# Dealing out a triangular solve over two chunks, with single-operation masks and a range check on one engine

## The chip, the cores and the metric

The kernel runs on one core of one Trainium2 chip. The metric is the device time of one execution in microseconds (us). TensorE (PE, matmuls), VectorE (DVE), ScalarE (ACT), GpSimd (POOL) and the DMA queue of SyncE (SP) each run their own instruction stream in order and wait for each other through semaphores.

## The reference

Three steps follow one another. The first is a recurrence with a state of 40 x 40 for each of 4 x 8 heads over 768 time steps; its output `y` goes through an MLP (320 to 2048 to 320), and that through a mixture of eight experts whose gates come from eight rounds of row and column normalisation.

```python
for t in range(S):                       # S = 768, state: [B=4, H=8, 40, 40]
    y[:, :, t] = einsum('bhd,bhde->bhe', rt, state)
    Sa = einsum('bhde,bhe->bhd', state, at)
    state = state * wt[:, :, None, :] - einsum('bhd,bhe->bhde', Sa, bt) \
            + einsum('bhd,bhe->bhde', vt, kt)
...
h = x @ w_in                             # 3072 x 320 @ 320 x 2048
g = where(h > 0, h, exp(min(h, 0)) - 1)
x = g @ w_out
...
for e in range(8):
    out += P[:, e:e+1] * (maximum(x @ w1[e], 0) @ w2[e])
```

## The kernel before

The 768 steps are cut into 24 chunks of 32. Within a chunk the recurrence becomes matmuls and, for each head, the solution of a 32 x 32 unit triangular system. Its coefficients come from a masked product (E3: matmuls, mask, store to DRAM as `Ad`, and step LT, which loads them as `LT` in the layout of the solve). The solve is `tsolve`: VectorE alternates a multiply (L417, `Tt<-Wk,LT`) and an update of `Wk` (L424) through 31 columns, 62 operations, for two chunks at once, and then SP stores `Wk` to DRAM (`Td`, L430) and loads it back transposed (`TT`, L434), the operand of the matmuls of step H2 (L463).

One turn of the main loop is one chunk c. A string in `PLAN["order"]` sets the order of its steps: prep (VectorE clamps and scans L312 to L322, GpSimd products L324, L333, L334, ScalarE's sum of squares L336 for the range check of w), E1 to E4, H1 to H4, O1 to O3b, `x` and `xl` (transposes of the finished y, `X` L576), and `m`, one unit of the first MLP (matmuls `ph` L588, ScalarE `m` L590 and L591, VectorE `g` L597, ScalarE `gh` L599, GpSimd `gl` L601, matmuls L615 to L619). O2 masks a product into `Gm` (L368), which O3b's matmuls (L545) read; O3a (L534) is between them; then comes VectorE's `xT` (L548). H3 ends with VectorE's `Y` (L494), which H4 (L503) reads.

At an even c, `T` creates the solve for chunks c+2 and c+3 and makes its first step, the start values of `Wk`. `G` allows it to be pumped from there on; every `p` then issues `PLAN["tp"]` operations of it, 3 in an even turn and 4 in an odd one. There are 16 places `p` in a turn. From c=4 on, the order on TensorE, VectorE, ScalarE and GpSimd is pinned as written; what stands on SP's queue, and everything before c=4 (`PLAN["start"]`), is ordered by a scheduler. After the last chunk, stage two runs the eight experts.

Of the kernel before, what the change touches and what calls it, by code (L numbers as in the profile page):

```python
# [98 lines left out]
def build(ctx, tc, r, k, v, w, a, b, w_in, w_out, wg, w1, w2, wa_d, kb_d, re_d, ro_d, vt_d, wp_d, consts, out, C, off):  # L99
# [140 lines left out]
    TTs = [r1.tile([128, H, 64], F32, name=f"TT{i}") for i in range(4)]  # L240
# [16 lines left out]
    def rec_init():  # L257
        for t in (wr, wq, dr, dq):
            V.memset(t, 0.0)
        work[1] = (early(1, "wr", [4 * NG, C + 1]), early(1, "wq", [4 * NG, C]), early(1, "dq", [4 * NG, C]), early(1, "aB", [NG * 2 * 2, 64]).rearrange("p (g u j) t -> p g u j t", u=2, j=2))  # L260
        for t in work[1]:
            G.memset(t, 0.0)
        V.memset(dr[:, :, 0], 1.0)
        for i in (3, 2):
            V.memset(bank[i], 0.0)
        for t in (aB, wmm, rB, *Ams, *TTs, Yw, Gm):
            G.memset(t, 0.0)
        for i in (0, 1):
# [134 lines left out]
    def tsolve(*cs):  # L403
        n = len(cs)
        LT2 = ltp[cs[0]][0]
        x0 = ltp[cs[0]][1]
        Wk = r1.tile([128, 2, CI, C], F32, tag="Wk", name="Wk")
        tmp = r1.tile([128, 2 * CI * (C - 1)], F32, tag="Tt", name="Tt")
        for x in range(n):
            G.tensor_copy(out=Wk[:, x].rearrange("p i t -> p (i t)"), in_=idk)  # L410
# [599 lines left out]
    with ExitStack():  # L1010
# [179 lines left out]
```

## Time and profile before

| | |
|---|---|
| device time, median of 3 runs | 2341.04 us (2337.09 to 2345.46) |
| profiled execution | 2338.0 us, span 2336.2 us |
| mean granted clock of TensorE | 0.976 |
| busy share of the span: PE, DVE, ACT, POOL | 92%, 43%, 31%, 22% |
| chain that ended last | PE 73%, DVE 15%, DMA 4% |

The span runs from the first to the last instruction. A share is a mean over stages: the start (to about 284 us) has the weight conversion and the first chunks, the middle (to about 825 us) the loop described above, and the rest the experts. The chain is followed back from the last instruction, each time to what released it. The granted clock is the share of TensorE's full speed (2.4 GHz) that it was given.

### The profile page before, as it was taken

To read this page: it belongs to the slowest core of one execution; us is meant where nothing else is said; L and a number is where in the kernel's file an instruction comes from. 1 tells how busy PE (TensorE), PEld (TensorE's weight loads), DVE (VectorE), ACT (ScalarE), POOL (GpSimd) and SP (SyncE) were. 2 spreads that over 40 slices of the span, in tenths; PEclk is the share of its full clock that TensorE was granted. 3 is DMA by queue.
4 is the path that set the end of the run, shared out by engine and by line. 5 is a ranking of instruction groups with operands and counts; after the bars stand their busy time and mean duration, and the time that the engine had idled before them with its cause. 6 is when DMAs were issued, how large, how long until landed. Compare 5 with 4: busy or idle time off the path is not lost.

```text
span 2336.2 us, 47201 instructions
## 1 busy us (share of the span) xinstructions
PE 2160.3 (92%) x19908; PEld 1967.2 (84%) x19908; DVE 1005.3 (43%) x2160; ACT 734.9 (31%) x1639; POOL 507.3 (22%) x608
## 2 busy tenths in 40 slices
PE   2376899999999999999999999999999999999998
PEld 2266888888888999899999999999999999999997
DVE  7888766666777522542222222222222222222222
ACT  3243455445455456323212112112112112112111
POOL 6344344434444326001002002002002002001000
PEclk9997899989999999999999999999999999999999
DMA  5353333333333214201001001001001001000000
GB/s 156 94 137 102 93 99 96 94 98 85 91 95 95 66 44 120 60 1 32 19 1 38 13 1 38 13 1 44 7 1 45 6 1 47 4 1 20 23 23 24
DMA packets 168452, 118.60 MB, mean 51 GB/s; under 512 B 102632, under 2 KB 148200, under 8 KB 168232
## 3 DMA queue, kind: packets, MB, share of 16 engines
q1 hardware_dynamic: 168232, 115.50, 18.5%
q8 instruction: 158, 2.59, 0.5%
q14 instruction: 62, 0.51, 0.1%
HBM read 96.97 MB, written 18.48 MB: 49 GB/s over the span
## 4 chain that ended last, share of the span: by engine, by line
PE 73%; DVE 15%; DMA 4%; ACT 3%; issue 2%; POOL 2%; SPq 1%; DVEq 0%; ACTq 0%; POOLq 0%
PE h L773 30%; PE pa L815 9%; PE pa L814 9%; PE pa L813 9%; PE ph L588 5%; DVE Tt L417 4%; DVE Wk L424 4%; PE a L615 1%; DVE g L597 1%; DMA WA<-in_wa 1%; PE a L616 1%; PE a L617 1%; PE P L364 1%; PE P L545 1%; DMA raw<-in_moe_w_out 1%
## 5 line engine op out<-in xcount | busy, mean ns | idle before, releaser
L773 PE MATMUL h<-X,a 128*128 128x512 f32 x3072 | 775.5, 394 | 0.0
L773 PEld LDWEIGHTS h<-X,a 128*128 128x128 f32 x3072 | 564.0, 188 | 102.8
L777 DVE SCALAR_TENSOR_TENSOR hl<-h,hh 128x512 fp32r<-128x512 f32 x384 | 264.8, 690 | 875.9 <-ACT hh L776 875.7
L776 ACT ACTIVATE hh<-h 128x512 fp32r<-128x512 f32 x384 | 230.0, 600 | 1021.2 <-PE h L773 1017.6
L814 PE MATMUL pa<-a,hl 128*128 128x320 f32 x1536 | 474.7, 310 | 0.0
L813 PE MATMUL pa<-a,hh 128*128 128x320 f32 x1536 | 472.1, 308 | 0.7 <-ACT acc L820 0.4
L815 PE MATMUL pa<-a,hh 128*128 128x320 f32 x1536 | 468.4, 309 | 0.0
L814 PEld LDWEIGHTS pa<-a,hl 128*128 128x128 f32 x1536 | 288.7, 188 | 16.0
L813 PEld LDWEIGHTS pa<-a,hh 128*128 128x128 f32 x1536 | 288.8, 188 | 15.6 <-ACT acc L820 0.8
L741 POOL TENSOR_TENSOR a<-rw,a 128x384 fp32r<-128x384 f32 x64 | 65.1, 1018 | 1057.8 <-ACT a L739 1050.5
L815 PEld LDWEIGHTS pa<-a,hh 128*128 128x128 f32 x1536 | 287.3, 188 | 0.0
L588 PE MATMUL ph<-X,Wt 128*128 128x256 f32 x1536 | 233.7, 296 | 16.0 <-DVE g L597 14.9
L601 POOL TENSOR_TENSOR gl<-g,gh 128x256 fp32r<-128x256 f32 x192 | 161.0, 839 | 381.0 <-ACT gh L599 278.5
L588 PEld LDWEIGHTS ph<-X,Wt 128*128 128x128 f32 x1536 | 202.6, 196 | 21.8 <-DVE g L597 17.1
L597 DVE SCALAR_TENSOR_TENSOR g<-m,ph 128x256 f32<-128x256 f32 x192 | 80.0, 416 | 176.8 <-ACT m L591 172.8
L417 DVE TENSOR_TENSOR Tt<-Wk,LT 128x120 f32<-128x120 f32 (+30 forms) x403 | 144.2, 358 | 25.7 <-POOL Wk L410 12.0
L424 DVE TENSOR_TENSOR Wk<-Wk,Tt 128x120 f32<-128x120 f32 (+30 forms) x403 | 145.5, 361 | 11.6
L824 DVE SCALAR_TENSOR_TENSOR acc<-pa,Pg,acc 128x320 f32<-128x320 f32 x168 | 84.3, 544 | 114.8 <-PE pa L815 114.8
L599 ACT ACTIVATE gh<-g 128x256 fp32r<-128x256 f32 x192 | 80.0, 417 | 163.4 <-DVE g L597 161.9
L590 ACT ACTIVATE m<-ph 128x256 f32<-128x256 f32 x192 | 73.2, 381 | 158.7 <-PE ph L588 156.6
L591 ACT ACTIVATE m<-m 128x256 f32<-128x256 f32 x192 | 80.1, 417 | 5.7
L615 PE MATMUL a<-gh,WoB 128*128 128x256 f32 x216 | 69.5, 322 | 1.3 <-ACT gh L599 1.3
(169 smaller groups left out, 2340.8 us busy)
## 6 DMA issues: line engine op xcount, KB each, us to landing
LT<-Ad SPq DMA_DIRECT2D x24, 512.0 KB
rw<-in_moe_w SPq DMA_DIRECT2D x64, 160.0 KB
WA<-in_wa SPq DMA_DIRECT2D x24, 416.0 KB
KE<-in_kb SPq DMA_DIRECT2D x24, 416.0 KB
rw<-in_moe_w SPq DMA_DIRECT2D x64, 128.0 KB
VU<-in_vt SPq DMA_DIRECT2D x24, 320.0 KB
raw<-in_wp SPq DMA_DIRECT2D x16, 384.0 KB
raw<-in_moe_w_out SPq DMA_DIRECT2D x16, 320.0 KB
```

Source lines behind the costliest of these rows:

```text
L417: V.tensor_tensor(out=tv, in0=Wk[:, 0:n, 0:ni, j:j + 1].to_broadcast(sh), in1=LT2[:, x0:x0 + n, j, j + 1:C].unsqueeze(2).to_broadcast(sh), ...
L424: dve["T"] = V.tensor_tensor(out=Wk[:, 0:n, 0:ni, j + 1:C], in0=Wk[:, 0:n, 0:ni, j + 1:C], in1=tv, op=ALU.subtract)
L588: T.matmul(ph, lhsT=Wt[0:kp, wi, 128 * f:128 * f + 128], rhs=X[0:kp, xi, :], start=(i == 0), stop=(i == 7))
L597: V.scalar_tensor_tensor(out=g, in0=m, scalar=-1.0, in1=ph, op0=ALU.add, op1=ALU.max)
L601: G.tensor_tensor(out=gl, in0=g, in1=gh.bitcast(F32), op=ALU.subtract)
L615: T.matmul(o, lhsT=Wo(f)[:, 128 * i:128 * i + 128], rhs=gh, start=(s and i == 0), stop=False, skip_group_check=True)
L773: T.matmul(h, lhsT=a1[:, wi, :], rhs=X[bk][:, xi, :], start=(i == 0), stop=(i == 7))
L776: A.activation(out=hh, in_=h, func=AF.Relu)
L777: V.scalar_tensor_tensor(out=hl, in0=h, scalar=0.0, in1=hh.bitcast(F32), op0=ALU.max, op1=ALU.subtract)
L813: T.matmul(o, lhsT=hh[:, ts_], rhs=a2[:, 0, :], start=(f == 0), stop=False)
L814: T.matmul(o, lhsT=hl[:, ts_], rhs=a2[:, 0, :], start=False, stop=False)
L815: T.matmul(o, lhsT=hh[:, ts_], rhs=a2[:, 1, :], start=False, stop=(f == NF2 - 1))
```

## The change

- The first operations of a solve are dealt earlier: `G` stands between the two halves of H3 in place of behind O2, and `PLAN["tp"]` alternates, 3 and 3 operations in an even turn, 2 and 3 in an odd one.
- The coefficients of three chunks lie in one tile, used in turn (`c % 3`), and LT always stands at its first place in the string. The start values of `Wk` come by a DMA from the constants, not by GpSimd copies; there are two `TT` tiles, not four.
- A mask is one VectorE operation over 128 partitions and 1024 elements that also writes the zeroes; the clearing of the mask tiles at the start is gone.
- The range check: GpSimd's subtraction L334 and ScalarE's Square are replaced by two ScalarE passes, Abs of w less the middle of the range, and Relu of that less half the range, summed.

```diff
-    "order": "lv E4 m prep+3 ldw+4 p E3+3 xl m E3+3 p H1 m p E2+3 LT+3 m p H2 lu+1 m prep+4 p E1+3 ldk+4 m prep+4 p x m T prep+4 p H3 m x H3 p O1 m O1 p H4 m YW+1 prep+4 p O2 x m O2 G p m x p O3a m prep+4 p O3b m O3b p m p m p LT+3 w",
+    "order": "lv E4 m prep+3 ldw+4 p E3+3 xl m E3+3 p H1 m p E2+3 LT+3 m p H2 lu+1 m prep+4 p E1+3 ldk+4 m prep+4 p x m T prep+4 p H3 m G x H3 p O1 m O1 p H4 m YW+1 prep+4 p O2 x m O2 p m x p O3a m prep+4 p O3b m O3b p m p m p w",
-    "tp": (3, 4),
+    "tp": ((3, 3), (2, 3)),
-    TTs = [r1.tile([128, H, 64], F32, name=f"TT{i}") for i in range(4)]
+    TTs = [r1.tile([128, H, 64], F32, name=f"TT{i}") for i in range(2)]
-        for t in (aB, wmm, rB, *Ams, *TTs, Yw, Gm):
+        for t in (aB, wmm, rB, *TTs, Yw):
             G.memset(t, 0.0)
...
-        G.tensor_tensor(out=wv, in0=wv, in1=wr[0:HR, :, 1:C + 1][:, :, ::-1], op=ALU.subtract)
-        yield
-        A.activation(out=wf, in_=wf, func=AF.Square, accum_out=wmm[0:HR, c:c + 1])
+        yield
+        A.activation(out=wf, in_=wf, func=AF.Abs, bias=wmid[0:HR])
+        A.activation(out=wf, in_=wf, func=AF.Relu, bias=whalf[0:HR], accum_out=wmm[0:HR, c:c + 1])
...
-        for bi in range(2):
-            p, q = slice(64 * bi, 64 * bi + 64), slice(C * bi, C * bi + C)
-            V.tensor_tensor(
-                out=dst[p].rearrange("p u h t -> p (u h) t")[:, :, q],
-                in0=PS[p, :].rearrange("p (h t) -> p h t", t=C),
-                in1=cc("mask")[p, q].unsqueeze(1).to_broadcast([64, 2 * H, C]),
-                op=ALU.mult,
-            )
+        V.tensor_tensor(
+            out=dst.rearrange("p u h (b t) -> p (u h) b t", b=2),
+            in0=PS.rearrange("p (h t) -> p h t", t=C).unsqueeze(2).to_broadcast([128, 2 * H, 2, C]),
+            in1=cc("mask").rearrange("p (b t) -> p b t", b=2).unsqueeze(1).to_broadcast([128, 2 * H, 2, C]),
+            op=ALU.mult,
+        )
...
-        LT2 = ltp[c - 1][0] if x else r1.tile([128, 2, C, C], F32, tag="LT", name="LT")
-        ltp[c] = (LT2, x)
-        SY.dma_start(out=LT2[:, x].rearrange("p s t -> p (s t)"), in_=dap(z.Ad, 0, [[C * C, B * H], [0, 4], [1, C * C]]))
+        SY.dma_start(out=LTs[:, c % 3].rearrange("p s t -> p (s t)"), in_=dap(st[c].Ad, 0, [[C * C, B * H], [0, 4], [1, C * C]]))
...
-        for x in range(n):
-            G.tensor_copy(out=Wk[:, x].rearrange("p i t -> p (i t)"), in_=idk)
+        SY.dma_start(out=Wk[:, 0:n].rearrange("p x i t -> p x (i t)"), in_=consts[:, nidk:nidk + CI * C].unsqueeze(1).to_broadcast([128, n, CI * C]))
...
-                        solve(PLAN["tp"][c % 2])
+                        pk += 1
+                        solve(PLAN["tp"][c % 2][pk % 2])
```

The line numbers of the changed kernel are a little lower: L417 becomes L412, L424 L419, L430 L425, L434 L429, L393 L389, L494 L489, L439 L434, L597 L592, L548 L543 on VectorE and L553 L548 on SP; the new Wk load is L405. The order of the matmuls in the loop stays as it was.

Place 1 is VectorE's stream in an even turn, from Y on: where a solve begins. Before:

```order
L494 TENSOR_TENSOR Y<-P_99,Yw 104x8x40
L494 TENSOR_TENSOR Y<-P_100,Yw 104x8x40
L597 SCALAR_TENSOR_TENSOR g<-m,ph 128x256
L439 COPY uE<-P_102 80x512
L597 SCALAR_TENSOR_TENSOR g<-m,ph 128x256
L368 TENSOR_TENSOR Gm<-P_101,cst 64x16x32 x2
L417 TENSOR_TENSOR Tt<-Wk,LT 128x62
L424 TENSOR_TENSOR Wk<-Wk,Tt 128x2x31
L417 TENSOR_TENSOR Tt<-Wk,LT 128x60
L576 TENSOR_TENSOR X<-P_102,X 128x3x128
```

The same stretch in the changed kernel, from the second Y on:

```order
L489 TENSOR_TENSOR Y<-P_100,Yw 104x8x40
L412 TENSOR_TENSOR Tt<-Wk,LT 128x62
L419 TENSOR_TENSOR Wk<-Wk,Tt 128x2x31
L412 TENSOR_TENSOR Tt<-Wk,LT 128x60
L592 SCALAR_TENSOR_TENSOR g<-m,ph 128x256
L434 COPY uE<-P_102 80x512
L419 TENSOR_TENSOR Wk<-Wk,Tt 128x2x30
L412 TENSOR_TENSOR Tt<-Wk,LT 128x58
L419 TENSOR_TENSOR Wk<-Wk,Tt 128x2x29
L412 TENSOR_TENSOR Tt<-Wk,LT 128x56
L419 TENSOR_TENSOR Wk<-Wk,Tt 128x2x28
L412 TENSOR_TENSOR Tt<-Wk,LT 128x108
```

Right behind these come g and the mask Gm, three further operations of the solve, and X: nine operations of the solve have moved ahead of Gm, from the odd turn.

Place 2 is VectorE's stream near the end of the odd turn, where a solve ends. Before:

```order
L597 SCALAR_TENSOR_TENSOR g<-m,ph 128x256
L368 TENSOR_TENSOR Gm<-P_101,cst 64x16x32 x2
L417 TENSOR_TENSOR Tt<-Wk,LT 128x32
L424 TENSOR_TENSOR Wk<-Wk,Tt 128x16x2
L417 TENSOR_TENSOR Tt<-Wk,LT 128x16
L424 TENSOR_TENSOR Wk<-Wk,Tt 128x16
L597 SCALAR_TENSOR_TENSOR g<-m,ph 128x256
L548 TENSOR_TENSOR xT<-P_101,xT 128x160
L548 TENSOR_TENSOR xT<-P_102,xT 128x160
```

And in the changed kernel:

```order
L592 SCALAR_TENSOR_TENSOR g<-m,ph 128x256
L368 TENSOR_TENSOR Gm<-P_101,cst 128x1024
L412 TENSOR_TENSOR Tt<-Wk,LT 128x70
L419 TENSOR_TENSOR Wk<-Wk,Tt 128x2x7x5
L412 TENSOR_TENSOR Tt<-Wk,LT 128x56
L419 TENSOR_TENSOR Wk<-Wk,Tt 128x2x7x4
L412 TENSOR_TENSOR Tt<-Wk,LT 128x48
L592 SCALAR_TENSOR_TENSOR g<-m,ph 128x256
L419 TENSOR_TENSOR Wk<-Wk,Tt 128x16x3
L412 TENSOR_TENSOR Tt<-Wk,LT 128x32
L543 TENSOR_TENSOR xT<-P_101,xT 128x160
L543 TENSOR_TENSOR xT<-P_102,xT 128x160
```

Ten operations of the solve stand behind Gm now, in place of four, and the last three come behind xT.

Place 3 is SP's queue from the end of one solve to the load of the coefficients for the next. Before:

```order
L430 DMA Td<-Wk 256x1x32 x6
L434 DMA TT_109<-Td 32x8x32 x4
L430 DMA Td<-Wk 256x1x32 x2
L553 DMA yd<-xT 128x384
L304 DMA rO<-in_ro 104x512
L434 DMA TT_110<-Td 32x8x32 x4
L287 DMA WA<-in_wa 104x1024
L565 DMA yt<-yd 128x384
L383 DMA Ad<-Am_118 32x8x32 x4
L393 DMA LT<-Ad 128x1x1024
L292 DMA KE<-in_kb 104x1024
```

In the changed kernel:

```order
L425 DMA Td<-Wk 256x1x32 x2
L548 DMA yd<-xT 128x384
L425 DMA Td<-Wk 256x1x32 x4
L429 DMA TT_109<-Td 32x8x32 x4
L425 DMA Td<-Wk 256x1x32 x2
L289 DMA WA<-in_wa 104x1024
L560 DMA yt<-yd 128x384
L429 DMA TT_110<-Td 32x8x32 x4
L383 DMA Ad<-Am_117 32x8x32 x4
L405 DMA Wk<-in_consts 128x2x256
L294 DMA KE<-in_kb 104x1024
L389 DMA LT<-Ad 128x1x1024
```

The store of y (yd) now stands among the stores of the solve, and the Wk load and the load of KE stand ahead of LT.

## Rows read from the trace of the kernel before

**Rows 1.** Busy time by window: us, then busy us (instructions) by engine, clock, DMA share, GB/s

```profile
core 0: us, PE busy (x) PEld busy (x) DVE busy (x) ACT busy (x) POOL busy (x), PEclk, DMA share, GB/s
284.00:825.00 541.00, 498.83 (x8533) 467.15 (x8533) 373.87 (x898) 272.57 (x703) 224.29 (x266) 0.96 0.35 90
825.00:2336.00 1511.00, 1496.44 (x8993) 1356.55 (x8991) 406.19 (x723) 361.58 (x696) 154.15 (x175) 1.00 0.08 24
```

**Rows 2.** Waits of TensorE from 284 to 825 us

```profile
engine line waited for: us in total, times, longest us
PE P L534 <- ACT m L591: 18.7, 9, 2.2
PE P L503 <- DVE Y L494: 9.3, 7, 1.3
PE ph L588 <- DVE g L597: 7.2, 8, 1.6
```

**Rows 3.** Timeline of TensorE, its waits in one pair of turns

```profile
start us, us, engine line op out<-in xcount [idle before <-releaser]
660.42 0.49 PE L534 MATMUL P<-Ss,rO 40*32 40x40 f32 x32 [0.64 <-DVE X L576]
...
682.34 1.22 PE L588 MATMUL ph<-X,Wt 128*128 128x256 f32 x8 [0.79 <-DVE g L597]
...
686.72 0.98 PE L503 MATMUL P<-cst,Yw 104*128 104x104 f32 x8 [1.33 <-DVE Y L494]
...
694.09 1.06 PE L534 MATMUL P<-Ss,rO 40*32 40x40 f32 x64 [2.20 <-ACT m L591]
```

**Rows 4.** Busy time by window around the odd turn of that pair

```profile
663.00:695.00 32.00, 27.68 (x485) 25.93 (x480) 30.14 (x75) 16.22 (x43) 13.30 (x15) 0.99 0.26 71
...
690.00:695.00 5.00, 2.80 (x80) 2.61 (x79) 4.65 (x14) 2.50 (x6) 1.74 (x2) 0.94 0.16 36
695.00:700.00 5.00, 5.00 (x62) 4.65 (x54) 0.97 (x3) 0.70 (x2) 4.16 (x5) 0.72 0.54 140
```

**Rows 5.** Timeline of VectorE, odd turn

```profile
662.70 0.79 DVE L548 TENSOR_TENSOR xT<-P,xT 128x160 f32<-128x160 f32 x2 [0.68 <-PE P L545]
...
665.13 1.14 DVE L424 TENSOR_TENSOR Wk<-Wk,Tt 128x104 f32<-128x104 f32 x1
...
666.52 0.25 DVE L417 TENSOR_TENSOR Tt<-Wk,LT 128x100 f32<-128x100 f32 x1
...
692.60 1.39 DVE L368 TENSOR_TENSOR Gm<-P,cst 64x512 f32<-64x512 f32 x2
```

**Rows 6.** Timeline of VectorE, even turn

```profile
652.42 0.88 DVE L494 TENSOR_TENSOR Y<-P,Yw 104x320 f32<-104x320 f32 x2
...
656.87 0.42 DVE L597 SCALAR_TENSOR_TENSOR g<-m,ph 128x256 f32<-128x256 f32 x1 [2.50 <-ACT m L591]
...
659.81 0.56 DVE L576 TENSOR_TENSOR X<-P,X 128x384 fp32r<-128x384 f32 x1
```

**Rows 7.** Timeline of GpSimd

```profile
655.19 1.25 POOL L456 TENSOR_TENSOR Yw<-Y,Wf 104x640 f32<-104x640 f32 x1
...
664.93 1.22 POOL L334 TENSOR_TENSOR WA<-WA,wr 104x512 f32<-104x512 f32 x1
```

**Rows 8.** The load of the coefficients: its issue on SP, and one on the chain

```profile
648.97 0.56 SPq L393 DMA_DIRECT2D LT<-Ad  x1
...
45.01 3.48 DMA LT<-Ad
```

**Rows 9.** Timelines and chain between the last step of a solve and H2

```profile
245.03 0.18 DVE L424 TENSOR_TENSOR Wk<-Wk,Tt 128x16 f32<-128x16 f32 x1
...
253.27 1.22 PE P L463 x30
...
632.23 1.45 PE L545 MATMUL P<-KB,Gm 128*64 128x40 f32 x32
...
644.30 0.90 PE L463 MATMUL P<-RH,TT 64*64 64x40 f32 x24
```

**Rows 10.** Timeline of ScalarE behind its pass L336 of the even turn

```profile
641.21 0.38 ACT L590 ACTIVATE m<-ph 128x256 f32<-128x256 f32 x1 [2.01 <-PE ph L588]
```

**Rows 11.** Start: timelines of GpSimd and of VectorE

```profile
12.37 3.52 POOL L334 TENSOR_TENSOR WA<-WA,wr 104x512 f32<-104x512 f32 x2
...
221.12 0.22 DVE L417 TENSOR_TENSOR Tt<-Wk,LT 128x62 f32<-128x62 f32 x1 [4.85 <-POOL Wk L410]
```

More of the change, by code (lines that the diff above doesn't have):

```diff
@@ L250, in build @@
     rB = r1.tile([128, NG, 2, 2, 64], F32, name="rB")
-    wmm = per.tile([128, NCH], F32, name="wmm")
+    wmm = per.tile([128, NCH + 2], F32, name="wmm")
+    wmid, whalf = wmm[:, NCH:NCH + 1], wmm[:, NCH + 1:NCH + 2]
     CI = C // 4
-    idk = r1.tile([128, CI * C], F32, name="idk")
     work = {None: (wr, wq, dq, aB)}
@@ L265, in rec_init @@
             V.memset(bank[i], 0.0)
-        for t in (aB, wmm, rB, *Ams, *TTs, Yw, Gm):
+        for t in (aB, wmm, rB, *TTs, Yw):
             G.memset(t, 0.0)
+        G.memset(wmid, -(WLO + WHI) / 2)
+        G.memset(whalf, 1e-5 - (WHI - WLO) / 2)
         for i in (0, 1):
@@ L384, in E3 @@
         z.Ad = Ad
-    ltp = {}
+    LTs = r1.tile([128, 3, C, C], F32, name="LT")
     def LT(c):
-        z = st[c]
-        x = c % 2
-        LT2 = ltp[c - 1][0] if x else r1.tile([128, 2, C, C], F32, tag="LT", name="LT")
-        ltp[c] = (LT2, x)
-        SY.dma_start(out=LT2[:, x].rearrange("p s t -> p (s t)"), in_=dap(z.Ad, 0, [[C * C, B * H], [0, 4], [1, C * C]]))
+        SY.dma_start(out=LTs[:, c % 3].rearrange("p s t -> p (s t)"), in_=dap(st[c].Ad, 0, [[C * C, B * H], [0, 4], [1, C * C]]))
     def E4(c):
@@ L404, in tsolve @@
         n = len(cs)
-        LT2 = ltp[cs[0]][0]
-        x0 = ltp[cs[0]][1]
+        x0 = cs[0] % 3
+        LT2 = LTs[:, x0:x0 + n] if x0 + n <= 3 else LTs[:, ::-2]
         Wk = r1.tile([128, 2, CI, C], F32, tag="Wk", name="Wk")
         tmp = r1.tile([128, 2 * CI * (C - 1)], F32, tag="Tt", name="Tt")
-        for x in range(n):
-            G.tensor_copy(out=Wk[:, x].rearrange("p i t -> p (i t)"), in_=idk)
+        SY.dma_start(out=Wk[:, 0:n].rearrange("p x i t -> p x (i t)"), in_=consts[:, nidk:nidk + CI * C].unsqueeze(1).to_broadcast([128, n, CI * C]))
         yield
@@ L419, in tsolve @@
                 in0=Wk[:, 0:n, 0:ni, j:j + 1].to_broadcast(sh),
-                in1=LT2[:, x0:x0 + n, j, j + 1:C].unsqueeze(2).to_broadcast(sh),
+                in1=LT2[:, :, j, j + 1:C].unsqueeze(2).to_broadcast(sh),
                 op=ALU.mult,
@@ L430, in tsolve @@
                 SY.dma_start(out=Td.rearrange("x (i q) t -> q x i t", q=4)[q], in_=Wk[q::4, x])
-            z.TT = TTs[c % 4]
+            z.TT = TTs[c % 2]
             for bb in range(B):
@@ L704, in check_w @@
         mm = c1.tile([128, 1], F32, name="mmw")
-        V.tensor_reduce(out=mm, in_=wmm, axis=AX.X, op=ALU.add)
+        V.tensor_reduce(out=mm, in_=wmm[:, 0:NCH], axis=AX.X, op=ALU.add)
         V.tensor_scalar(out=mm, in0=mm, scalar1=0.0, scalar2=None, op0=ALU.is_le)
@@ L1013, in build @@
         SY.dma_start(out=cst, in_=consts[:, 0:ncst])
-        SY.dma_start(out=idk, in_=consts[:, nidk:nidk + CI * C])
         SY.dma_start(out=wgs[:, 0:2, :], in_=wg[0:256, :].rearrange("(k p) e -> p k e", p=128))
@@ L1117, in build @@
                     step("T" if n == "t" else n, cs[0])
-        acc = 0
+        acc = pk = 0
         for c in range(2, NCH + 1):
@@ L1136, in build @@
                     try_xprep(n == "xl")
-                elif n == "LT":
-                    if not pump:
-                        advance(n, c + o)
                 elif n == "T":
```

2 rows, old and new, of the table PLAN are left out of this document.

## The prediction

> **What bounds the kernel now.** I read the busy times by stage first, then TensorE's waits in the stage with the gaps, then the timeline around one of each wait, and only then the other engines there. The last stage, after 825 us, is 1496 of 1511 us TensorE at full clock [rows 1]; the change doesn't touch it. The middle stage, 284 to 825 us, has 499 of 541 us of TensorE at a mean granted clock of 0.96 [rows 1]: here the recurrence runs two chunks per turn, woven with the first MLP. TensorE's waits there come in a few kinds only [rows 2]: 18.7 us at L534 in 9 waits, 9.3 at L503 and 7.2 at L588 behind g, 35.2 us together.
>
> One turn shows where they sit. In the odd chunk TensorE stops 0.79 us for g, 1.33 for Y and 2.20 before L534 [rows 3]. The last is put down to ACT's m, but L534 starts at 694.09, just when VectorE's second Gm mask ends (692.60 plus 1.39, [rows 5]); L545 reads Gm right behind, in the same step of the order, so I take the mask as the releaser. VectorE is busy 30.1 of 32 us in this odd chunk [rows 4], with solve steps between everything else: it is the bound of this stretch, and only of it. In the even chunk it has 2.50 us idle before one g [rows 6].
>
> Behind the 2.20 us wait the granted clock falls: 0.94 in the five us with the wait, 0.72 in the next five [rows 4], so toward the lower level (1.2 of 2.4 GHz). That costs 5 x (0.06 + 0.28) = 1.7 us per turn. Nine waits make 15 us; the stage's mean says 541 x 0.04 = 22, rounded. I use 19. The waits of 0.64 in the even chunk, and of 0.79 and 1.33 in the odd one [rows 3], come before the fall, with 0.99 as mean of the 32 us around them [rows 4].
>
> **Part by part.** *Solve steps dealt anew.* 62 steps per pair: 18 in the even and 44 in the odd chunk before, 27 and 35 after. Between the even chunk's xT and the odd chunk's Gm stand 15 fewer steps: 9 at the front, and 6 at the end, now behind Gm (order, places 1 and 2). An undisturbed step there takes 0.25 us and the next begins at about 0.29 [rows 5]; 9 x 0.3 + 6 x 0.25 = 4.2 us.
>
> *Range check off GpSimd.* L334 took 1.22 us on GpSimd from 664.93, and the step that began at 665.13 took 1.14 in place of 0.25 [rows 5, 7]. Without L334 that is 0.9 us back, or nothing if the multiply before it merely moves there. ScalarE gets one more pass per chunk over the same tile, bounded by GpSimd's 1.22 us for it; right after its old pass it waits 2.01 us for TensorE [rows 10], which covers that. Without the cover m and then g would be up to 1.2 us later.
>
> *One mask operation.* Two of 512 elements end in 1.39 us; two xT additions of 160 took 0.79 [rows 5]: 0.85 ns per element by that slope, so one of 1024 is 1.13, against no saving at all as the other bound. I take 1.2, a gain of 0.2.
>
> Together 4.2 + 0.9 + 0.2 = 5.3 us; Gm would begin at 687.3. With no waits TensorE would come to that L534 at 694.09 - 2.20 - 1.33 - 0.79 = 689.77, and bring Gm's input 2.1 us earlier than before, which then sets Gm to about 687.7 and its end to 688.9: 0.9 us to spare. If L334's 0.9 stays, the spare is near nothing, but no wait of note comes. So the odd waits go: **-35 us**, and with the 2.20 wait the fall of the clock: **-19 us**.
>
> *What the even chunk pays.* Nine more steps are 2.3 us, into an idle time of 2.50 [rows 6]. But the first step needs the coefficient load LT. It was issued at 648.97 before [rows 8]; in the new order the Wk load and the solve's end stand ahead of it on the queue of SP (order, place 3), which I put at three issues of LT's own 0.56 us, 1.7 in all; with 3.5 us for the load (an early one, [rows 8]) it lands near 654.2, while VectorE comes to the step when Y is done, at 653.3 [rows 6]. Behind that step in VectorE's order are g, uE, the other steps, Gm, and then, after three further ones, X, for which L534 already waits 0.64 us [rows 3]. X begins at 659.81 now [rows 6], also behind three steps; 0.9 of waiting and 2.3 of steps, less 2.5 of idle and 0.2 of the mask, gives +0.5 for X. Two of the moved steps also meet GpSimd's Yw (1.25 us at 655.19, [rows 7]); if it holds them as L334 held its step, X is 0.9 later still. The bounds for this wait are no growth and +1.4 per turn; I take 0.8, eight times: **+6 us**.
>
> Row 665.13 shows a two-input VectorE operation lasting exactly as long as the GpSimd operation beside it runs on [rows 5, 7]. The Trainium skill ("SBUF — State Buffer", section "SBUF: two separate sides") says that the port pair shared by VectorE and GpSimd is locked for a whole instruction, for VectorE operations with two SBUF inputs against a GpSimd operation that reads SBUF. That speaks against moving steps into GpSimd's Yw; by the rule alone the even term would be the 1.4 bound, 11 us in place of 6.
>
> *Coefficients to H2.* The last step now stands behind xT in the odd chunk. The path from last step to H2 took 253.27 - 245.21 = 8.1 us early in the run [rows 9]. L545 ends at 633.68 and H2 begins at 644.30 [rows 9]: 10.6 us. Less xT 0.8, three steps 0.6, the yd store issued between the Td stores 0.5 leaves 8.7 against 8.1, and part of the 10.6 was slow clock that goes. So it is thin: between 0 and 0.8 us of wait, **+3 us** for eight turns.
>
> *Wk by a load, two TT tiles, ring of three.* The load replaces a copy on GpSimd; its time lies under LT's, counted above. Only the first step of a solve waits for either. A TT tile is read by H2 before the next solve of the same parity ends. Nothing.
>
> *The first pair and a remainder:* c=4 isn't yet in step; one wait with its fall of the clock may stay: **+2 us** (one of 2.2 plus 1.7, half likely). *Start, before 284 us:* two L334 (3.52 us, [rows 11]) and some memsets are gone ahead of the first keys, worth 0 to 3.5 us; the solve that begins at 221.12 after 4.85 us idle [rows 11] waits for a load (3.5 us as a bound by LT, [rows 8]) in place of a copy, and its order is moved past a mask: 0 to 3.5 lost. I take **-1**.
>
> Sum: -35 - 19 + 6 + 3 + 2 - 1 = -44. The profiled execution took 2338.0 us (span 2336.2), 3.0 below the median of the three runs: 2338 - 44 = **2294**.
>
> **Rivals.** *The waits move to the even chunk.* LT lands late and Yw holds steps: X is 1.4 later, L534 waits 2.0 us, and the clock falls there in place of the odd chunk. 8 x (0.6 + 1.7) = 18 more: 2312. For it: the idle time is nearly used up. Against: 0.5 follows from undisturbed rows.
>
> *The clock keeps falling though the waits are short.* Several small waits per turn stay by the terms above. Against it speak those of 0.64, 0.79 and 1.33 that left it high [rows 3, 4]. If not: 8 x 1.7 = 14, 2308. The Trainium skill ("TensorE: Matmul & The Clock Gate", section "A second HAM failure mode: psum-queue depth-cycling") has frequent micro-idles between groups of matmuls as enough to make the clock go up and down.
>
> *Slower: the coefficients come late for H2.* Td, TT and yd share SP's queue with the loads, in order. From the forecast, 44 / 8 = 5.5 us per turn, with a fall of the clock 3.8 of wait, are needed to lose everything. If yd's wait for xT holds the four Td stores and TT behind them, H2 comes 6 us late: 8 x (6 + 1.7) = 62, 2356. Against: the spare of about 0.6 would have to be wrong by 4.
>
> *No change.* Gm isn't the releaser of L534, and the steps only change place: the odd waits stay, 2338.
>
> *Better.* X not later, the start's gain whole: 2338 - 35 - 22 - 3 = 2278.
>
> **How the numbers follow.** Forecast (2283 to 2303) 0.52; waits in the even chunk 0.24; clock 0.07; better 0.05; slower 0.07; no change 0.05. The range, 2278 to 2320, holds the first four: about 0.85. About 0.3% (7 us) is what a measurement here tells from no change: faster 0.88, same 0.05, slower 0.07.
>
> **What would show it.** In 284 to 825: the waits at L534's, L503's and L588's counterparts in the odd chunk under 0.4 us, mean clock 0.99 or more, the stage about 43 us shorter. Masks of 1.2 us in one row. The first step of a solve waiting about 1 us for LT or Wk, and X's wait near 1.2 in the even chunk. Wrong would be: a wait of 2 us at any place in each turn, H2 waiting for TT, or an odd L534 that still starts when Gm ends.

## The result and the profile after

The changed kernel took 2352.81 us against 2336.99 us (medians of 14 runs each): 1.006 times as long, 95% interval 1.0049 to 1.0071. The forecast was 2294. The profiled execution has a span of 2350.8 us, 14.6 more than before. The first matmul of the expert stage stands at 894.44 us before and at 903.01 after, so 8.6 us are lost ahead of that stage and 6.0 within it, though the diff changes no matmul of it.

The 8.6 us don't lie in the eight pairs of turns from chunk 4 to chunk 19. Counted from the first matmul of H2 (L463 before, L458 after), these take 523.2 us before and 522.9 after: the odd turns are 46.5 us shorter in all (288.8 to 242.3), the even ones 46.1 longer (234.5 to 280.6). Lost are 4.5 us ahead of chunk 4's H2 (252.3 and 256.8) and 4.4 between chunk 20's H2 and the expert stage, where the last solve begins in the same late way (turn 20 takes 27.7 us before and 33.1 after).

The same two views as in [rows 1] and [rows 2], busy time by window and TensorE's waits from 284 to 825 us:

```profile
core 0: us, PE busy (x) PEld busy (x) DVE busy (x) ACT busy (x) POOL busy (x), PEclk, DMA share, GB/s
0.00:284.00 284.00, 158.05 (x2188) 136.17 (x2188) 212.53 (x514) 101.60 (x230) 112.20 (x143) 0.66 0.44 118
284.00:825.00 541.00, 501.22 (x8580) 469.08 (x8578) 373.26 (x861) 289.11 (x731) 208.03 (x235) 0.97 0.37 95
```

```profile
engine line waited for: us in total, times, longest us
PE P L366 <- DVE uE L434: 16.6, 7, 3.0
PE P L529 <- ACT m L585: 5.6, 7, 0.8
PE P L529 <- DVE X L571: 4.5, 7, 0.7
PE P L529 <- ACT m L586: 3.5, 3, 1.3
PE P L458 <- DMA TT<-Td: 3.4, 7, 0.8
```

The start's clock, 0.66 here and 0.89 in the trace before, belongs to the execution and not to the kernel: in the sixteen traces of this document it is 0.66 to 0.69 in six and 0.86 to 0.89 in ten, and chunk 4's H2 starts at 251.5 to 262.7 us in the six and at 250.4 to 257.3 in the ten.

The waits of the odd turn are gone or short, as forecast: nothing for Y or g, and 0.8 us left ahead of O3a (L529, before L534). In their place TensorE waits up to 3.0 us for uE, in the even turn. The next three views follow one pair of turns: TensorE's rows, a window of five us, and VectorE in the even turn.

```profile
649.40 0.28 PE L458 MATMUL P<-RH,TT 64*64 64x40 f32 x2 [0.65 <-ACT m L585]
649.84 1.09 PE L458 MATMUL P<-RH,TT 64*64 64x40 f32 x30 [0.16 <-DMA TT<-Td]
...
664.16 0.69 PE L366 MATMUL P<-rB,uE 80*64 80x64 f32 x16 [2.16 <-DVE uE L434]
...
683.08 1.13 PE L458 MATMUL P<-RH,TT 64*64 64x40 f32 x32
...
699.56 0.78 PE L529 MATMUL P<-Ss,rO 40*32 40x40 f32 x64 [0.81 <-ACT m L585]
...
713.81 1.50 PE L458 MATMUL P<-RH,TT 64*64 64x40 f32 x32 [0.57 <-DMA TT<-Td]
```

```profile
664.00:669.00 5.00, 4.84 (x67) 4.64 (x67) 4.76 (x12) 3.55 (x9) 2.73 (x3) 0.66 0.16 36
```

```profile
657.78 0.88 DVE L489 TENSOR_TENSOR Y<-P,Yw 104x320 f32<-104x320 f32 x2
662.44 0.22 DVE L412 TENSOR_TENSOR Tt<-Wk,LT 128x62 f32<-128x62 f32 x1 [3.78 <-DMA LT<-Ad]
...
663.43 0.68 DVE L434 COPY uE<-P 80x512 f32<-80x512 f32 x1
...
664.94 1.18 DVE L419 TENSOR_TENSOR Wk<-Wk,Tt 128x58 f32<-128x58 f32 x1
...
667.18 1.22 DVE L368 TENSOR_TENSOR Gm<-P,cst 128x1024 f32<-128x1024 f32 x1
```

The first step of the solve waits 3.78 us for LT, with g, uE and Gm behind it on VectorE; TensorE waits 2.16 us for uE, and the granted clock falls to 0.66 in the five us behind that. From one H2 (L458) to the next, the even turn shown takes 33.7 us and the odd one 30.7. Before, the matmuls of L463 began at 644.30 [rows 9] and at these times, so the turns took 29.4 and 35.4:

```profile
673.73 1.13 PE L463 MATMUL P<-RH,TT 64*64 64x40 f32 x32
...
709.15 1.13 PE L463 MATMUL P<-RH,TT 64*64 64x40 f32 x32
```

The pair is about as long as it was: the loss has changed turns.

Why LT is late, from SP's queue:

```profile
650.15 1.79 SPq L429 DMA_DIRECT2D TT<-Td  x4
651.99 2.19 SPq L383 DMA_DIRECT2D Ad<-Am  x4
654.25 0.43 SPq L405 DMA_DIRECT2D Wk<-in_consts  x1
654.77 0.38 SPq L294 DMA_DIRECT2D KE<-in_kb  x1
655.62 0.56 SPq L389 DMA_DIRECT2D LT<-Ad  x1
```

LT is issued at 655.62 and the step starts at 662.44, 6.8 us later; the prediction had taken 3.5 for the load. Its 512 KB stand behind 256 KB of start values and 416 KB of KE. Means of the eight even turns, counted from H2's start, give the whole of it: LT is issued at 7.9 us (5.0 before), the step starts at 13.8, and it waits 3.7 us. The issue is late because of the Ad store ahead of it, which LT reads back: the mask that makes its data ends at least 3.0 us ahead of H2, but the store is issued behind the solve's last TT load, here 2.6 us behind H2's start (before: 0.1 us ahead of it).

The expert stage shows its loss in the distance of its units (8 matmuls of L768, L773 before, and 12 more). Block 0 of the tokens, then block 1, in the changed kernel; then block 1 before:

```profile
1468.61 2.00 PE L768 MATMUL h<-X,a 128*128 128x512 f32 x8
1472.20 1.09 PE L768 MATMUL h<-X,a 128*128 128x512 f32 x4
...
1497.34 2.04 PE L768 MATMUL h<-X,a 128*128 128x512 f32 x8
1500.98 2.04 PE L768 MATMUL h<-X,a 128*128 128x512 f32 x8
```

```profile
1487.08 2.02 PE L773 MATMUL h<-X,a 128*128 128x512 f32 x8
1490.70 2.02 PE L773 MATMUL h<-X,a 128*128 128x512 f32 x8
```

A unit of block 0 takes 3.59 us in both kernels (before: 1458.35 to 1461.94), one of block 1 takes 3.61 to 3.62 before and 3.64 after, at full clock and with TensorE never idle. Blocks 2 to 5 do as block 1. The change also adds two columns to the tile `wmm`, which holds the range check's sums; the cut diff ahead of the prediction doesn't show it. They move every tile behind it in SBUF by 32 bytes: the inputs X1 to X5 of blocks 1 to 5 start at 896 in place of 864 modulo 2048 bytes of a partition (reckoned from the tiles' sizes; no view shows addresses). X0, at the other end, didn't move.

### The profile page after: what moved, and what is told of

Read it like the earlier page. It is cut to its first block, busy times and chain, and to the rows that moved or that the text cites. A ratio compares the mean times of both kernels' runs of the same rounds, so it can differ in the third digit from the quotient of the medians.

```text
span 2350.8 us, 47073 instructions
## 1 busy us (share of the span) xinstructions
PE 2172.9 (92%) x19908; PEld 1973.5 (84%) x19908; DVE 997.7 (42%) x2112; ACT 755.3 (32%) x1663; POOL 476.4 (20%) x556
## 4 chain that ended last, share of the span: by engine, by line
PE 76%; DVE 10%; DMA 7%; SPq 2%; issue 2%; ACT 1%; POOL 1%; DVEq 0%; ACTq 0%; POOLq 0%
PE h L768 31%; PE pa L808 10%; PE pa L810 10%; PE pa L809 10%; PE ph L583 5%; DVE Wk L419 2%; DVE Tt L412 2%; PE a L610 2%; DMA WA<-in_wa 1%; DMA yt<-yd 1%; DMA Wk<-in_consts 1%; PE P L540 1%; PE a L611 1%; PE a L612 1%; SPq L425 1%
## 5 line engine op out<-in xcount | busy, mean ns | idle before, releaser
L768 PE MATMUL h<-X,a 128*128 128x512 f32 x3072 | 781.4, 396 | 0.2 <-DVE X L571 0.2
L768 PEld LDWEIGHTS h<-X,a 128*128 128x128 f32 x3072 | 564.2, 188 | 107.2 <-DVE X L571 0.4
L596 POOL TENSOR_TENSOR gl<-g,gh 128x256 fp32r<-128x256 f32 x192 | 168.8, 879 | 409.1 <-ACT gh L594 318.4
L583 PE MATMUL ph<-X,Wt 128*128 128x256 f32 x1536 | 238.7, 300 | 5.6 <-DVE g L592 5.6
L583 PEld LDWEIGHTS ph<-X,Wt 128*128 128x128 f32 x1536 | 208.3, 201 | 10.2 <-DVE g L592 6.2
L412 DVE TENSOR_TENSOR Tt<-Wk,LT 128x120 f32<-128x120 f32 (+30 forms) x403 | 141.3, 351 | 53.1 <-issue 18.0
L419 DVE TENSOR_TENSOR Wk<-Wk,Tt 128x120 f32<-128x120 f32 (+30 forms) x403 | 157.5, 391 | 9.2 <-DVE Tt L412 0.2
L592 DVE SCALAR_TENSOR_TENSOR g<-m,ph 128x256 f32<-128x256 f32 x192 | 80.0, 417 | 153.0 <-ACT m L586 148.9
```

The lines of the kernel that those rows point to most:

```text
L412: V.tensor_tensor(out=tv, in0=Wk[:, 0:n, 0:ni, j:j + 1].to_broadcast(sh), in1=LT2[:, :, j, j + 1:C].unsqueeze(2).to_broadcast(sh), op=ALU. ...
L583: T.matmul(ph, lhsT=Wt[0:kp, wi, 128 * f:128 * f + 128], rhs=X[0:kp, xi, :], start=(i == 0), stop=(i == 7))
L596: G.tensor_tensor(out=gl, in0=g, in1=gh.bitcast(F32), op=ALU.subtract)
L768: T.matmul(h, lhsT=a1[:, wi, :], rhs=X[bk][:, xi, :], start=(i == 0), stop=(i == 7))
```

## The experiments

The theories are these. *Late supply:* the first step was moved 5 us forward and its loads weren't. *Overfull:* the nine steps ahead of Gm are too many by themselves. *Placement:* the 32 bytes cost the expert stage its 6 us. Ratios are to the kernel before, run beside each, with their 95% interval. Line numbers shift by a few from kernel to kernel.

**e1, constants placed back.**

```diff
-    wmm = per.tile([128, NCH + 2], F32, name="wmm")
+    wmm = per.tile([128, NCH], F32, name="wmm")
...
+    flagt = per.tile([128, 8], F32, name="flag")     # was [1, 1], 32 bytes all the same
+    wmid, whalf = flagt[:, 1:2], flagt[:, 2:3]
```

> The changed kernel with the two constants of the range check in an unused part of the 32 bytes of the flag tile, so that the tile of sums has 24 columns again and every tile behind it starts 32 bytes lower, as before the change. Theory (placement): the rows of blocks 1 to 5 in the expert stage show TensorE slower by a constant pattern, block 0, whose input tile did not move, shows none; so the 7 us of that stage come from the 32 bytes: about 2346 us against 2353, the stage from its first L773 counterpart to the end as long as before. Rival (the execution): the rate of that stage belongs to the run and not to the kernel: 2353, and the stage stays 7 us longer or varies.

2343.49 us, ratio 1.001 (0.9996 to 1.0024), so 0.5% less than the changed kernel. Placement holds. What is left of the change is neither gain nor loss. The eight pairs take 520.8 us here and chunk 4's H2 starts at 252.0, where the trace above has 522.9 and 256.8; so the 4.5 us lost ahead of that H2 aren't in every execution.

**e2, 32 bytes in the kernel before.**

```diff
+        c1.tile([128, 8], F32, name="pad")
         X += [c1.tile([128, 5, 512], F32R, name=f"X{i}") for i in range(1, NBLK)]
```

> The kernel before, with 32 unused bytes ahead of the input tiles X1 to X5 of the expert stage and nothing else changed; the first stage is untouched. Placement: 7 us more, about 2344 us. Rival (the execution, or one of the other moved tiles): 2337, no change.

2351.09 us, ratio 1.0046 (1.0029 to 1.0064), where 2344 was expected. Its units of block 1 stand as in the changed kernel, 3.64 us apart:

```profile
1495.39 2.04 PE L773 MATMUL h<-X,a 128*128 128x512 f32 x8
1499.03 2.04 PE L773 MATMUL h<-X,a 128*128 128x512 f32 x8
```

So it is none of the tiles ahead of X1 to X5. The tiles behind them moved here too; e8 tells these apart.

**e8, five starts in one kernel.**

```diff
-        X += [c1.tile([128, 5, 512], F32R, name=f"X{i}") for i in range(1, NBLK)]
+        for i, p in zip(range(1, NBLK), (16, 8, 264, 8, 256)):
+            if p:
+                c1.tile([128, p], F32, name=f"pad{i}")
+            X.append(c1.tile([128, 5, 512], F32R, name=f"X{i}"))
```

> The kernel before with the input tiles of blocks 1 to 5 of the expert stage at five other starts (modulo 2048 bytes 928, 960, 2016, 0 and 1024, by unused bytes between them). Placement: each block gets a pattern of its own in the pitch of its eight matmuls, the same in all its units; the block at 2016, where block 0 lies, has block 0's (1.612 us for seven pitches, against 1.628 and 1.640). Rival (something else of the moved tiles): all blocks alike. The time is between 2325 and 2350 us.

2339.2 us, ratio 1.0001 (0.9981 to 1.002). X3, at 2016 as X0, has X0's distance of 3.59 us:

```profile
1545.55 2.00 PE L773 MATMUL h<-X,a 128*128 128x512 f32 x8
1549.14 2.00 PE L773 MATMUL h<-X,a 128*128 128x512 f32 x8
```

By the starts of their first matmuls, eight units take 28.73 us in X0 and X3, 28.88 in X1 (928 modulo 2048) and 28.95 in X2, X4 and X5 (960, 0 and 1024); before, X1 to X5 took 28.91. Each block has the pace of its own start, so it is X's tiles and not the others. Placement holds again; no rule over all starts is claimed from these few.

**e3, KE behind LT.**

```diff
-        SY.dma_start(out=z.KE[0:HR]...)
+        d = SY.dma_start(out=z.KE[0:HR]...)
+        if c >= 8 and c % 2 == 0:
+            tc.add_manual_dep(d.ins, lts[-1].ins.name, <order only>)
```

> The changed kernel with the even turns' load of KE held behind the load of the coefficients LT on SP's queue (an order alone). Theory (LT late): LT waits for the 416 KB of KE and the 256 KB of the start values ahead of it; without KE it lands 1.5 to 2 us earlier, the first step's wait falls from 3 to about 1.3 us, TensorE's wait behind uE and Gm from 2.2 to about 0.5, and the clock stays up in the even turn: 8 x 3.3 = 26 us less, about 2327. Rival (overfull): the nine steps more are too many for the even turn in any case; the waits move from uE to Gm and stay near 1.5 to 2 us, the clock still falls: 2345 to 2353.

2346.05 us, ratio 1.0029 (1.0015 to 1.0044): 7 us less than the changed kernel, not 26. LT is issued 8.1 us behind H2's start (mean of the eight even turns), 7.9 in the changed kernel: KE's issue was not what it waited for. It reads what the Ad store writes, and that store comes late (e7). The step now starts 4.9 us behind LT's issue in place of 5.9, and still waits 2.8 us in place of 3.7. In the turn whose H2 starts at 642.68:

```profile
651.07 0.56 SPq L392 DMA_DIRECT2D LT<-Ad  x1
```

**e4, start values by GpSimd.**

```diff
+    idk = r1.tile([128, CI * C], F32, name="idk")
...
-        SY.dma_start(out=Wk[:, 0:n]..., in_=consts[...])
+        for x in range(n):
+            G.tensor_copy(out=Wk[:, x].rearrange("p i t -> p (i t)"), in_=idk)
```

> The changed kernel with the start values of the solve copied by GpSimd from a tile again, not loaded (and with the constants of the range check placed as in the first experiment, for room, which by the placement theory is 7 us by itself). LT late: 256 KB and one issue less ahead of LT, so it lands 1 to 1.5 us earlier; the wait at uE falls to about 1 us and the clock mostly stays up: 16 to 24 us less and 7 for the place, 2322 to 2330. Overfull: 2340 to 2346.

2338.01 us, ratio 0.9989 (0.9977 to 1.0002): 0.2% less than e1, and the two intervals overlap. The step starts 5.0 us behind LT's issue (6.0 in e1) and waits 2.7 us (3.6). So each of the two loads ahead of LT is worth about 1 us of the wait, and both experiments left the theories apart by too little.

**e5, the same steps dealt 5 us later** (with e1's and e3's edits).

```diff
-    "order": "... H3 m G x H3 p O1 m O1 p H4 m YW+1 prep+4 p O2 ..."
+    "order": "... H3 m x H3 p O1 m O1 p H4 m G YW+1 prep+4 p O2 ..."
-    "tp": ((3, 3), (2, 3)),
+    "tp": ((4, 4), (2, 3)),
```

> The changed kernel with the solve's first step dealt later: G stands behind H4, ahead of YW, and an even turn deals 4 operations at each of its 7 places left, 28 in place of 27 in all; with KE held behind LT as in the third experiment and the constants placed as in the first. Four steps, not nine, stand ahead of Gm. LT late (the need moved ahead of the supply): the first step now stands about 5 us later in the turn, behind uE, and LT is there; the even turn's waits fall to about 1 us and the clock stays up in both turns, with the odd turn's steps still thinned: 65 us per pair become 60 to 61, 8 x 4 to 5 less, 2300 to 2312. Overfull (steps ahead of Gm and X, whatever LT does): the waits stay near 2 us, 2330 to 2340.

2305.09 us, ratio 0.9849 (0.9826 to 0.9872). The waits of its middle stage, none above 1.4 us:

```profile
PE P L533 <- DVE X L575: 6.9, 8, 1.0
PE P L533 <- ACT m L589: 4.6, 6, 0.8
PE P L533 <- ACT m L590: 2.4, 2, 1.4
```

LT is not there, though it was expected to be: the first step still waits for it, up to 3.0 us. But uE stands ahead of the step on VectorE now, and TensorE waits for uE nowhere in this stage:

```profile
633.25 0.22 DVE L416 TENSOR_TENSOR Tt<-Wk,LT 128x62 f32<-128x62 f32 x1 [2.99 <-DMA LT<-Ad]
```

The mechanism of the forecast, steps taken out of the odd turn, is worth having; the place in the even turn was what spoiled it. Late supply and overfull both allow this.

**e6, the old dealing in the changed kernel** (with e1's edit).

```diff
-    "order": "... H3 m G x H3 ... O2 x m O2 p m ..."
+    "order": "... H3 m x H3 ... O2 x m O2 G p m ..."
-    "tp": ((3, 3), (2, 3)),
+    "tp": ((3, 3), (4, 4)),
```

> The changed kernel with the old dealing alone (G behind O2, 3 operations per place in an even turn and 4 in an odd one) and the constants placed as in the first experiment; one-operation masks, the range check without GpSimd, the ring and the loads stay. LT late: the first step has 5 us more and doesn't wait, and the odd turn gets its waits back, less what masks and range check give (1.1 us ahead of Gm): L534's counterpart waits 1.1 to 2.0 us in place of 2.2 and the clock falls in some turns: 2320 to 2337. Rival (the loads or the two TT tiles cost by themselves): slower than before, above 2345.

2313.24 us, ratio 0.9892 (0.9865 to 0.992), better than expected. Everything in the change but the dealing gains 1.1% (25 us); the dealing where it stands costs 1.2% (28 us) against this (e1). The wait ahead of O3a is still 2.04 us in each odd turn, but behind six of the eight the clock stays at 1.00, as here:

```profile
610.60 0.78 PE L530 MATMUL P<-Ss,rO 40*32 40x40 f32 x64 [2.04 <-ACT m L587]
```

```profile
610.00:615.00 5.00, 4.40 (x116) 4.20 (x117) 2.20 (x8) 1.14 (x4) 3.44 (x4) 1.00 0.18 29
615.00:620.00 5.00, 5.00 (x87) 4.62 (x87) 0.85 (x3) 3.64 (x9) 1.85 (x4) 1.00 0.30 46
```

**e7, the new dealing alone, in the kernel before** (the order and `tp` of the diff and nothing else).

> The kernel before with the new dealing alone (G between the halves of H3, 3 and 3, 2 and 3); start values by GpSimd, one pair tile for the coefficients, masks and range check as before. LT late: the solve ends later, so the stores, Ad and LT come later on SP's queue, and the first step, 5 us earlier, waits 2 to 3 us for LT here too; the even turn's waits replace the odd turn's: 2335 to 2345. Rival (the new loads alone are at fault): LT is in time, the waits vanish, 2300 to 2315.

2358.75 us, ratio 1.0094 (1.0066 to 1.0122), more than expected. The first step waits for LT here too (2.8 us on average), where neither the Wk load nor the ring exists; the new loads are not the cause by themselves. LT is issued 8.3 us behind H2's start, 5.0 in the kernel before, and the last issue of the Ad store ahead of it comes at 6.4 in place of 1.4. Its data are ready 3.4 us and more ahead of H2, so what holds it is SP's queue, where it stands behind the stores and TT loads of a solve that now ends later: the new dealing delays the load that it wants sooner. No run moved that store.

```profile
665.89 0.23 DVE L417 TENSOR_TENSOR Tt<-Wk,LT 128x62 f32<-128x62 f32 x1 [1.93 <-DMA LT<-Ad]
```

**e9, no step ahead of the even turn's Gm** (e6 with another table).

```diff
-    "tp": ((3, 3), (4, 4)),
+    "tp": ((3, 4, 5, 5, 5, 5), (2, 3)),      # one entry per place p
```

> The changed kernel with G at its old place (behind O2), and at the six places left in an even turn 3, 4, 5, 5, 5 and 5 operations, 27 as in the changed kernel; odd turns 2 and 3; constants placed as in the first experiment. No step stands ahead of the even turn's Gm. LT late: the first step has 5 us more, LT is there, the even turn stays at 28.6 to 29.4 us as with the old dealing and the odd one at 30.1 to 30.7 as with the new: 59.5 per pair against 61.3 and 61.8 in the fifth and sixth, 2290 to 2302. Overfull (27 operations are too many for an even turn wherever they stand): the even turn grows by what the odd one loses, 2305 to 2320.

2307.77 us, ratio 0.9851 (0.9827 to 0.9876), the stage's clock at 1.00. The intervals of e5 and e9 lie on each other; the 2290 to 2302 were not reached. The odd turns take 30.9 us on average and the even ones 30.3, not 28.6 to 29.4: a part of what overfull expected, though no step stands ahead of Gm.

**e10, e9 with X1 to X5 where X0 lies.**

```diff
+        c1.tile([128, 288], F32, name="pad")
         X += [c1.tile([128, 5, 512], F32R, name=f"X{i}") for i in range(1, NBLK)]
```

> The ninth kernel with X1 to X5 moved by 1152 unused bytes, to 2016 modulo 2048 bytes, where block 0 lies. Placement: seven pitches sum to 1.612 to 1.615 us in every block in place of 1.627, the stage is 320 x 8 x 0.002 = 5 us shorter than the ninth. Rival: block 0's pattern belongs to that block and not to the start: no difference to the ninth.

2303.58 us, ratio 0.9827 (0.9804 to 0.985): the fastest, 1.7% below the kernel before. All blocks have 3.59 us per unit, here block 1:

```profile
1458.34 2.00 PE L769 MATMUL h<-X,a 128*128 128x512 f32 x8
1461.93 2.00 PE L769 MATMUL h<-X,a 128*128 128x512 f32 x8
```

The difference to e9 (4 us) is smaller than the intervals; the traces show it (the expert stage takes 1433.9 us, 1440.7 in e9), the times alone don't.

**e11, e6 with GpSimd's subtraction and Square again.**

```diff
+        G.tensor_tensor(out=wv, in0=wv, in1=wr[...], op=ALU.subtract)
         yield
-        A.activation(out=wf, in_=wf, func=AF.Abs, bias=wmid[0:HR])
-        A.activation(out=wf, in_=wf, func=AF.Relu, bias=whalf[0:HR], accum_out=...)
+        A.activation(out=wf, in_=wf, func=AF.Square, accum_out=...)
```

> The sixth kernel (old dealing) with the range check as before: GpSimd's subtraction and one Square. Shared port (the subtraction holds a step of the solve for 0.9 us per chunk): Gm of the odd turn comes 0.9 us later, the 2.0 us wait ahead of O3a grows to about 2.9, the clock falls again: 8 x (0.9 + 1.7) = 21 us more, 2334. Rival (the subtraction lies beside work that doesn't need the port, or the step is held by something else in its place): 2313, as the sixth.

2338.81 us, ratio 0.9976 (0.9959 to 0.9992): 20 us of the 25 that e6 gains are gone. The size is as expected, the place isn't: the wait ahead of O3a stays as in e6, TensorE waits for g again (4.2 us in 7 waits), and the clock falls behind six of the eight odd waits, two in e6. Length times the share of the clock that is missing, added up over the eight pairs, is 24 us here and 8 in e6; the pairs are 15 us longer. In this trace a further 11 us lie ahead of chunk 4's H2 (262.7 and 251.5), and why stays open. One of the six:

```profile
634.37 0.78 PE L530 MATMUL P<-Ss,rO 40*32 40x40 f32 x64 [2.03 <-ACT m L587]
```

```profile
635.00:640.00 5.00, 5.00 (x67) 4.67 (x55) 1.07 (x4) 0.42 (x1) 4.05 (x4) 0.66 0.24 39
```

**e12, e6 with two mask operations again.**

```diff
+        for t in (aB, wmm, rB, *Ams, *TTs, Yw, Gm):
...
-        V.tensor_tensor(out=dst..., in0=PS..., in1=mask..., op=ALU.mult)     # 128 x 1024
+        for bi in range(2):
+            V.tensor_tensor(out=dst[p]...[:, :, q], in0=PS[p, :]..., in1=mask[p, q]..., op=ALU.mult)
```

> The sixth kernel (old dealing) with two mask operations again (and the cleared tiles they need). Small part: the masks take 1.39 us in place of 1.22, the wait ahead of O3a goes from 2.04 to 2.2 us in the odd turn: 8 x 2 x 0.17 = 3 us, 2316. If the clock turns on that 0.2 us, it falls again in each odd turn: 8 x (0.2 + 1.7) = 15 us, 2328.

2337.05 us, ratio 0.9974 (0.996 to 0.9987): 19 us more than e6 for 0.17 us per mask (the clearing of the mask tiles at the start is back too). The wait is 2.21 us, and the clock falls behind seven of the eight: by the same sum as in e11 that takes 31 us. One of them:

```profile
636.05 0.78 PE L532 MATMUL P<-Ss,rO 40*32 40x40 f32 x64 [2.21 <-ACT m L589]
```

```profile
640.00:645.00 5.00, 5.00 (x34) 4.79 (x30) 0.74 (x2) 1.22 (x3) 1.75 (x3) 0.60 0.36 56
```

**e13, LT without its wait, the dealing as changed** (e1's edit too).

```diff
-    "order": "lv E4 ...
+    "order": "LE+3 lv E4 ...                  # LE: LT at the head of a turn, from c = 5 on
...
-        SY.dma_start(out=LTs[:, c % 3]..., in_=dap(st[c].Ad, 0, ...))
+        SY.dma_start(out=LTs[:, c % 3]..., in_=dap(w1 if c > 5 else st[c].Ad, 0, ...))
```

> The first kernel (the changed one with the constants placed back) with the new dealing untouched, but LT, from chunk 6 on, read from a tensor of the inputs of the same size, so that it waits for no Ad store and is issued about a turn earlier; the solve's coefficients are therefore not the right ones, all instructions, shapes and orders on the four pinned engines stay. LT late: the first step waits for nothing or, at most 1 us, for the start values; uE, Gm and X come 3 us earlier, TensorE waits less than 1 us at any place of the even turn and the clock stays up: 35 us per even turn become 30 to 31, 8 x 4 to 5 less than the first kernel, 2300 to 2312. Overfull (nine steps ahead of Gm are too many by themselves): the waits ahead of O3a stay at 1.3 and 0.7 us, the clock falls in most even turns, 2328 to 2343.

2339.37 us, ratio 0.9966 (0.9949 to 0.9984), 0.4% less than e1. With LT there the step still waits 1.7 us on average, now for the other load, the start values: 9.7 us in 6 waits in that stage. The supply has two halves, and either alone is late.

**e14, neither load ahead of the first step** (e13 with e4's edit).

> The thirteenth kernel (LT from an input tensor, about a turn earlier, so that its coefficients are not the right ones) with the start values copied by GpSimd as in the fourth, so that the first step waits for neither load. Supply late (LT and, behind it, the start values): the first step waits under 0.7 us, uE and Gm wait for nothing that TensorE feels, X's wait stays near 0.7; the clock stays up in the even turn, 30 to 31 us in place of 34 to 36: 2298 to 2312. Overfull (the nine steps by themselves): O3a still waits 1.3 us for Gm and 0.7 for X and the clock falls in most even turns: 2328 to 2340.

2330.21 us, ratio 0.9957 (0.9941 to 0.9973), within what overfull expected. The first step starts with Y's end, and O3a still waits for Gm and X; VectorE, then TensorE:

```profile
648.20 1.29 DVE L415 TENSOR_TENSOR Tt<-Wk,LT 128x62 f32<-128x62 f32 x1
...
651.76 1.18 DVE L422 TENSOR_TENSOR Wk<-Wk,Tt 128x58 f32<-128x58 f32 x1
...
654.00 1.22 DVE L370 TENSOR_TENSOR Gm<-P,cst 128x1024 f32<-128x1024 f32 x1
```

```profile
655.37 0.49 PE L532 MATMUL P<-Ss,rO 40*32 40x40 f32 x32 [1.17 <-ACT m L589]
656.66 0.49 PE L532 MATMUL P<-Ss,rO 40*32 40x40 f32 x32 [0.80 <-DVE X L574]
```

So both theories hold a part. From 1.001 (e1) to 0.9957 the supply made early is worth 0.5%, 12 us; from there to e5's 0.9849 lie another 1.1%, 25 us. Not all of these are the steps' own place: in e13 and e14 H2 waits 7.7 and 9.0 us for TT, 2.6 in e1 and 1.6 in e5, so moving LT has a price of its own. Which part is the larger stays open. Of the nine steps two last a microsecond longer beside a GpSimd operation, one beside aE (1.29 us) and one beside Yw (1.18); the step between them takes 0.22.

## Why the prediction was wrong

**The step that failed** is "What the even chunk pays": +0.8 us per turn, 6 in all. The even turns became 46.1 us longer, 5.8 each, of which 3.4 are waits of TensorE and 2.4 the slower clock. Three terms of the step were mis-sized.

- *The wait for LT* was put at 0.9 us and is 3.7 on average. Counted from H2's start, LT was to be issued at 6.4 us and to land at 9.9, with Y done at 9.0; measured are 7.9, 13.8 and 10.1. So the load is 2.4 us short (5.9 against 3.5): it was priced by one early row, though the order showed Wk and KE ahead of it. The issue is 1.5 us short: the prediction counted issues, and not that the Ad store, which LT reads, stands behind the TT loads of a solve that ends later (e7).
- *The steps held by GpSimd* were 0.9 us of the bound, and the value held only a part of that; e14 shows two of about 1 us.
- *The delay* was followed only to X. uE stands behind the first step too, and TensorE waits for it 2.16 us in the turn shown, from where the clock falls in the even turn.

The prediction's first rival (waits move to the even chunk, the clock falls there) is the mechanism that came, at 2312 and 0.24, though ahead of uE's reader and not of L534; its price was too small because it used the same wait for LT.

**The odd turn** was right. Y's and g's waits are gone, and O3a's went from 2.20 to 0.81, 0.4 above what the forecast allowed. The odd turns are 46.5 us shorter, where -35, -19 and +3 make 51. What failed is that the clock's 19 us came back: the fall moved to the even turn, and the stage has 0.97 in place of 0.96.

**"The last stage ... the change doesn't touch it"** was wrong by 6 us. No matmul of it changed, but the start of its input tiles did (e1, e2, e8). From the pace of eight units, 28.91 us before and 29.12 after, forty such passes (eight experts, five blocks) make 8. The prediction had no step that asked what the diff's tile sizes move in SBUF.

**Masks** were right in time, 1.22 against 1.2, and wrong in worth: 0.2 us in the forecast, 19 us in e12 with the old dealing, most of it slower clock. The range check is alike: forecast 0.9 us ahead of Gm; e11 shows 20 us, but with O3a's wait unchanged, so by another way (g, the clock and the start) than the one given.

**H2's coefficients** were right: 3.4 us in 7 waits, forecast 3. **Start:** -1 was forecast. Chunk 4's H2 starts 4.5 us later in the changed kernel's trace; the eight traces with its start unaltered have 251.3 to 257.2 us, the four with the old start 250.4 to 253.2. So no gain is seen, and the loss is not clear of the spread.

**The lock of the shared port**, as the Trainium skill has it ("SBUF — State Buffer", section "SBUF: two separate sides"), was put into the bound only; the trace of e14 agrees with it (1.29 us beside GpSimd's aE of 1.28, 1.18 beside Yw of 1.26) and it belonged in the value. **The clock:** the fall after waits that are no longer than others is told in the last section; frequent micro-idles as enough for it, which the Trainium skill has ("TensorE: Matmul & The Clock Gate", section "A second HAM failure mode: psum-queue depth-cycling"), are neither shown nor refuted by these runs.

## What to carry to other kernels

When a consumer is moved forward, price its loads by what their issue waits for and by what stands ahead of them on the queue, and follow everything in order behind the consumer, not only the one that waited before. Moving work from one turn to the next can also delay the stores that feed the moved work. Two parts of a change can be worth 1% together and little alone: without the range check or without the masks, 20 of e6's 25 us are gone. And compare the start of every tile of the hot stage before and after, since a few bytes in a tile that lives long move them all.

## What the runs showed that was not expected

TensorE's pace at full clock depends on where the moving operand starts in SBUF: 3.59, 3.61 to 3.62 and 3.64 us per unit of 20 matmuls at 2016, 864 and 896 modulo 2048 bytes. Eight units take 29.12 us in the three traces with X1 to X5 at 896 and 28.91 in the eleven at 864. Why these starts differ, whether it is the start alone or its distance to the weights, stays open.

The length of a wait alone does not decide whether the clock falls behind it. In the kernel before, each of the eight odd turns waits 2.1 to 2.2 us ahead of L534 and the clock falls each time. In e8, whose loop is the same code, the same waits of 2.20 to 2.21 us leave it at 1.00 in five turns of eight, as here:

```profile
502.41 0.78 PE L534 MATMUL P<-Ss,rO 40*32 40x40 f32 x64 [2.20 <-ACT m L591]
```

```profile
505.00:510.00 5.00, 5.00 (x74) 4.77 (x71) 1.47 (x4) 2.14 (x6) 4.24 (x5) 1.00 0.53 131
```

With waits of 2.04 us it falls in two turns of e6 and in six of e11. What decides stays open, so a price per wait, as the prediction used it, is an average at best.
